# Weight conversion with signs made on GpSimd, and a first output product in two passes

## The chip, the cores and the metric

The kernel runs on one core of a Trainium2 chip. The metric is the device time of one execution in microseconds (us). A core has five engines that work side by side, each through its own queue in order: TensorE (PE) multiplies matrices, VectorE (DVE) and ScalarE (ACT) work elementwise and can read the banks of PSUM in which TensorE leaves its sums, GpSimd (POOL) works elementwise between tiles of on-chip memory (SBUF), and SyncE (SP) issues DMAs.

## The reference

Eight batches of twelve heads, 448 tokens and head size 64 go through attention with normalised queries and keys, and the result, as 3584 rows of 768, through a gated feed-forward layer with 1536 hidden values. The three weight matrices come as 64-bit floats.

```python
q_n, k_n = rmsnorm(q, g_q), rmsnorm(k, g_k)
attn = softmax(q_n @ k_n.T / sqrt(64))
x = (attn @ v).transpose(0, 2, 1, 3).reshape(3584, 768)
g = x @ w_gate                       # 768 x 1536
silu = g * (1.0 / (1.0 + exp(-g)))
out = (silu * (x @ w_val)) @ w_out   # 1536 x 768
```

## The kernel before

The work is cut into four blocks of two batches. A block has twelve pairs of heads (m = 0 to 47 in all, `attention`, L703), a hidden product (gate and value) and an output product (`block`, L1267).

**Products.** Each large product is done by a bilinear scheme on 3 x 3 sub-blocks by 15 products in place of 18 per two batches. Both factors are first combined into 15 "sides": sums and differences of blocks. The hidden product of a block runs over four groups g of hidden columns, and within each over the 15 products x in the order `UP_ORDER`, for gate and value, each two terms deep (`up_product`, L1280). Every product is left in a PSUM bank and read from there at once, by ScalarE if it opens a sum (COPY) and by VectorE if it is added to or subtracted from one (L1242 to L1248). The bank is free for the next product when that read is done. The output product (`down_product`, L1452) has the 15 products of `DOWN_ORDER`, for two halves s of the columns, each four terms deep: its terms are the groups g. Two banks serve it, one for each s. Its data sides are made by `combine` (L1425) from the hidden values in `gt` into the tiles `gt`, `hs` and two spare slots of `xs`; sums 6 and 1 are made group by group behind the hidden product and wait in block 0 for the last use of `hs` by a conversion. The data sides of the hidden product are made in `xs` by `sides` (L1042), after the last pair of a block's half.

**Weights.** Twenty-four pieces of weights, 16 for the hidden product (four to a group) and 8 for the output product (two to a group), are converted by `convert` (L1101). A piece is 128 x 1152 64-bit numbers. It is loaded into one of nine places, which are tiles not needed yet (`gt`, `hs`, `es`, `xs`, `work` of the pairs' inputs, `spare`); ScalarE scales the high word into a 32-bit number (L1127) and turns the low word into a correction (L1131); VectorE rounds in two halves of three operations each (`round_part`, L1138): a shift (L1147), the sign bit masked out of the high word and joined (L1150), and the correction added (L1153). GpSimd makes the sums among the blocks in twelve operations (L1171, L1174), and the 15 sides are stored to DRAM (L1199), in `up_sides` per group or in `down_sides`. From there SP loads them piece by piece into two `ws` buffers just ahead of TensorE (`load_sides`, L1250). With `by_bank` the results of the first two vector operations go to a PSUM bank of the pool `st` instead of back to SBUF. The pieces are handed out in rounds (L1586 on): 6 in the first round, during the first twelve pairs, then 10, 6 and 2, all planned before the end of block 0's hidden product. Each round walks over its own list of places, and a place is taken again when its store has landed. Pairs 12 and on use `work` and `es`, so their loads wait for the last conversion in `work` and their scores for the last in `es`.

**Order.** The order in which instructions stand in the engines' queues comes from a planner (`Order`, L361). Every piece of work is added with an engine, an expected duration, a due time (`when`), what it must follow, and buffers that it takes. `run` (L422) keeps a clock for each engine in this model and places at each step the piece that could start first, by due time among those close together. `port=True` keeps VectorE and GpSimd pieces from being planned at the same time. Due times come from a few numbers at L636: the first pair at `LEAD` = 14 us and each of the first twelve at a distance `PAIR` = 10 us, then block 0's hidden product with 20 us of extra room, and so on. What really happens follows the queues and the semaphores, not the due times.

The first twelve pairs run before block 0, and the twelve of a next block run between the output product's pieces of the block before. Pairs need TensorE for scores (L840), weighted values (L916) and row sums (L940); the early ones also to spread the reciprocals (L980).

Of the kernel before, what the change touches and what calls it, by code (L numbers as in the profile page):

```python
# [9 lines left out]
F32 = mybir.dt.float32  # L10
# [467 lines left out]
def fast(  # L478
# [87 lines left out]
    def take(name, key, shape):  # L566
# [4 lines left out]
        if name in OFTEN:  # L571
            at = OFTEN[name] + order.turn[name] % BUFS[name]
            tiles[name, key] = spare[:, ts(at, S)]
            return tiles[name, key]
        if name == "eh":
            at = order.turn["eh"] % BUFS["eh"]
            tiles[name, key] = more[:, at].rearrange("p (h q) -> p h q", h=2)
            return tiles[name, key]
# [35 lines left out]
    down_sides = dram.tile([P, 15, 2, NG, P], F32, name="down_sides")  # L614
# [21 lines left out]
    LEAD, PAIR = 14.0, 10.0  # L636
# [66 lines left out]
    def attention(m):  # L703
# [296 lines left out]
        def divide():  # L1000
# [4 lines left out]
            "ACT", 0.55, when + 3.0, copy_sums, after=[last, up_done.get(b // 2 - 1)], uses=at[:1]  # L1005
# [36 lines left out]
    def sides(n, c, when):  # L1042
# [7 lines left out]
        for i, one, two, op in (  # L1050
# [13 lines left out]
            free = down_products.get((n - 1, 11), []) if i in (11, 12) else []  # L1064
            last = [
# [35 lines left out]
    def convert(key, src, sums, to, when, place, by_bank):  # L1101
# [9 lines left out]
        wait = [last_exp[0]] if place in (ES, PAIRS, GT[2]) else []  # L1111
# [21 lines left out]
        )  # L1133

# [3 lines left out]
        def round_part(k, takes=False):  # L1138
            if by_bank:
                if k == 0:  # L1140
                    take(*bank, [P, 2, TB])
                part = ts(k, VALUES // 2)
                to = tiles[bank].rearrange("p b t -> p (b t)")[:, 0 : VALUES // 2].bitcast(U32)
            else:
                part = ts(k, VALUES // 2)
                to = bits[:, part]
            nc.vector.tensor_scalar(  # L1147
                out=to, in0=bits[:, part], scalar1=3, scalar2=None, op0=ALU.logical_shift_left
            )
            nc.vector.scalar_tensor_tensor(  # L1150
                to, hi[:, part], 0x80000000, to, op0=ALU.bitwise_and, op1=ALU.bitwise_or
            )
            nc.vector.tensor_tensor(out=bits[:, part], in0=to, in1=lo[:, part], op=ALU.add)  # L1153

        last = one
        for k in range(2):
            last = add(
                "DVE", 2.28 if by_bank else 1.85, when, lambda k=k: round_part(k), after=[last, two],
                takes=[bank] if by_bank and k == 0 else [], uses=[bank] if by_bank and k else [],
                port=not by_bank,  # L1160
            )
# [51 lines left out]
    def down_weights(i, *how):  # L1213

        g, s = divmod(i, 2)
        w = moe_w_out.rearrange("(k g p) (n s f) -> p k g n s f", g=NG, p=P, n=3, s=2)
        weights["down", i] = convert(
            ("down", i), lambda k, n: w[:, k, g, n, s], DOWN_SUMS, down_sides[:, :, s, g], *how
        )
# [3 lines left out]
    down_done = {}  # L1223
    last_load = []
# [25 lines left out]
    def load_sides(key, sides, part, sums):  # L1250

        size = 2 * (NC2 if sums is UP_SUMS else NG) * P
        to = take(*key, [P, WS])[:, 0 : len(part) * size].rearrange("p (x f) -> p x f", f=size)
        i = 0
        for names, first in ((sums, 0), (BLOCKS, len(sums))):
            here = sorted(names.index(x) for x in part if x in names)
            if here:
                size = len(here)
                src = sides[:, ds(first + here[0], size)]
                nc.sync.dma_start(to[:, ds(i, size)], src.rearrange("p x a b f -> p x (a b f)"))  # L1260
                i += size
# [5 lines left out]
    def block(n):  # L1267
# [122 lines left out]
        def up_load(g, piece):  # L1390
# [3 lines left out]
                lambda: load_sides(key, up_sides[g], UP_ORDER[5 * piece :][:5], UP_SUMS),  # L1394
# [6 lines left out]
        for g in range(NG):  # L1401
# [5 lines left out]
        up_done[n] = last  # L1407
        bank_read[:] = [free[0, 0], free[0, 1]]
# [3 lines left out]
        raw = [gt[:, :, k] for k in range(6)]  # L1412
        a1, a2, a3, b1, b2, b3 = raw
        h0, h1 = hs[:, 0], hs[:, 1]
# [3 lines left out]
            6: h0, 1: h1, 10: h2, 14: b1, 2: h0, 3: h1, 0: a3, 11: h2, 4: b3, 12: h0, 5: a1, 8: h1,  # L1418
            7: b2, 13: b1, 9: a2,
        }  # L1420
        all_hidden = [hidden[g, k] for g in range(NG) for k in range(6)]
# [3 lines left out]
        def combine(x, one, two, op, when, after, g=None):  # L1425
            to = where[x]
            if g is not None:
                to, one, two = to[:, g], one[:, g], two[:, g]
            done = add(
                "DVE", 0.64 if g is not None else 2.05, when,  # L1430
                lambda: combined(to, one, two, op), after=after, port=True,
            )
            made.setdefault(x, []).append(done)
            return done

        span = (BOTH if n < NB - 1 else DOWN) / 15

        def step_time(x):
            return block_end(n) + DOWN_ORDER.index(x) * span

        for g in range(NG):
            when = start + 30 * (g + 1) * unit + 1.0
            before = [down_done.get(n - 1)] + ([staged[HS]] if n == 0 else [])
            combine(6, a1, a2, None, when, [hidden[g, 0], hidden[g, 1], *before], g)
            combine(1, b2, h0, ALU.subtract, when, [made[6][g], hidden[g, 4], *before], g)
        combine(10, h1, b1, None, block_end(n) + 3.0, [*all_hidden, *made[1], up_done[n]])
# [5 lines left out]
        def down_product(step, x, s):  # L1452
            nonlocal last
            when = step_time(x) + s * span / 2
            piece = step // 2
            key = ("ws", (n, "o", piece))
            size = 2 if piece < 7 else 1
            if piece not in loads:
                loads[piece] = add(
                    "SP", 0.9, when - 24.0,  # L1460
                    lambda: load_sides(key, down_sides, DOWN_ORDER[2 * piece :][:2], DOWN_SUMS),
                    after=[*last_load, *(weights["down", i] for i in range(2 * NG))], takes=[key],
                    kb=512 * size, early=10.0,
                )
                last_load[:] = [loads[piece]]
            fresh = x in FRESH

            def emit():
                w = tiles[key][:, 0 : 4 * NG * P]
                w = w.rearrange("p (x s g f) -> p x s g f", s=2, g=NG, f=P)  # L1470
                at = place_of(x, DOWN_ORDER[step - step % 2 :][:2], DOWN_SUMS)
                for g in range(NG):
                    nc.tensor.matmul(  # L1473
                        banks[s][:, 0:S], w[:, at, s, g], where[x][:, g],
                        start=fresh and g == 0, stop=g == NG - 1, skip_group_check=True,
                    )

            last = add(
                "PE", 2 * PRODUCT, when, emit,
                after=[  # L1480
                    last, loads[piece], bank_read[s], *made.get(x, []),
# [5 lines left out]
            when += 2 * PRODUCT  # L1487
            t, how, *final = DOWN_READ[x]
            name = "vw"[s] + {"t0": "0", "t1": "1", "t4": "2", "t3": "3", "d": "3", "t5": "4"}[t]
            value = (name, (n, "o", t))  # L1490
# [15 lines left out]
            if x == 12:  # L1506
                other = ("vw"[s] + "1", (n, "o", "t1"))
# [7 lines left out]
            if not final:  # L1515
                return
# [24 lines left out]
        for step, x in enumerate(DOWN_ORDER):  # L1541
            when = step_time(x)
            for s in range(2):
                down_product(step, x, s)
            after = {
                6: [(2, b3, b1, ALU.subtract, (1,))],
                1: [(3, h0, a3, ALU.add, (2, 10))],
                10: [(11, a3, b3, ALU.add, ()), (4, b2, b3, None, (2, 11))],
                14: [(13, a2, b2, ALU.add, (2, 10))],
                2: [(12, h1, a1, ALU.subtract, (3,))],  # L1550
                3: [(8, a3, b2, ALU.subtract, (12,)), (9, a2, a3, ALU.add, (6, 13))],
            }.get(x, [])
            for to, one, two, op, others in after:
                combine(
                    to, one, two, op, when + span,
                    [*all_hidden, *products[n, x], *(d for o in others for d in made[o])],
                )
# [28 lines left out]
    turns = [(*XS, *GT[:2], HS, SPARE), (ES, PAIRS, GT[2], SPARE, HS), (ES, PAIRS, HS, SPARE), (ES, HS)]  # L1586
    starts = [LEAD - 4.0, FIRST - 20.0, FIRST + 60.0, FIRST + 110.0]
    spans = [16.0, 8.0, 9.0, 10.0]
    counts = [6, 10, 6, 2]
    todo = iter(first)  # L1590
    for n in range(4):
        for i in range(counts[n]):
            make, index = next(todo)
            make(index, starts[n] + spans[n] * i, turns[n][i % len(turns[n])], n > 0)
# [72 lines left out]
```

## Time and profile before

| | us |
|---|---|
| median of 3 runs | 1500.53 (1499.26 to 1501.53) |
| the profiled execution | 1499.07 |
| its span in the profile | 1497.2 |
| TensorE busy | 1434.6 |
| VectorE busy | 916.9 |
| ScalarE busy | 689.8 |
| GpSimd busy | 408.8 |

How to read it: a row of the slices is a busy share in tenths for 40 equal parts of the span, and PEclk in the same way the clock that TensorE was granted. A line such as `PE mm L1299 <- DVE gt L1248: 9.9, 2, 6.7` says that TensorE's instructions of line 1299 which write `mm` waited for VectorE's of line 1248 which write `gt`, 9.9 us in all, twice, 6.7 at most. A line of the timeline has start, duration, engine, line, operation, tile written and tiles read, shapes, count, and in brackets the idle time before it. Every matmul in 32 bits leaves two records. Stages by TensorE's work: first pairs from 14.66 to 149.3 us, block 0's hidden product to 353.9 and its output product with the next pairs to 526.4; then 717.9 and 872.1 for block 1, 1064.1 and 1218.4 for block 2, 1399.5 and 1485 for block 3, which has no pairs left to run.

### The profile page before, as it was taken

The page shows a single profiled execution, that of the slowest core. Times are in us where ns is not written, and L with a number is a line of the kernel's source. Part 1 is how long each engine was busy: PE and PEld are TensorE (multiplying, and loading weights), DVE is VectorE, ACT ScalarE, POOL GpSimd, SP SyncE. Part 2 cuts the span into 40 slices and gives each one's busy share as a digit, 9 for nine tenths or more (in the row PEclk, how much of TensorE's full clock was granted, in tenths as well). Part 3 has the DMA queues.
Part 4 walks back from the last instruction along what each step waited for, and adds up shares of the span by engine and source line. Part 5 has one row for each costly group of instructions (what it writes and reads, how often), then busy time and mean ns, then how long its engine had stood idle before and what let it go on. Part 6 is the DMA issues. An engine that isn't in the chain of part 4 may idle for free.

```text
span 1497.2 us, 19504 instructions
## 1 busy us (share of the span) xinstructions
PE 1434.6 (96%) x6672; PEld 681.5 (46%) x6672; DVE 916.9 (61%) x1405; ACT 689.8 (46%) x1372; POOL 408.8 (27%) x468
## 2 busy tenths in 40 slices
PE   5898999799999999999999999999999999999998
PEld 2333444343344455554444445554444445555553
DVE  5867877868886743455876753453786854423533
ACT  6764544347777422254777432235677532122100
POOL 2562666544454300002344400002344410000000
PEclk9898999999999999999999999999999999999999
DMA  7675999974444342343453442343344343222235
GB/s 168 152 160 166 315 309 309 288 219 99 98 99 109 80 137 71 114 114 88 100 123 82 87 130 84 104 118 104 82 110 109 83 114 106 71 106 70 84 97 106
DMA packets 415922, 193.31 MB, mean 129 GB/s; under 512 B 324164, under 2 KB 397892, under 8 KB 409668
## 3 DMA queue, kind: packets, MB, share of 16 engines
q1 hardware_dynamic: 402688, 190.35, 47.5%
q10 hardware_dynamic: 12996, 1.61, 0.7%
q8 instruction: 55, 0.90, 0.3%
q14 instruction: 55, 0.45, 0.1%
q0 software_dynamic: 128, 0.00, 0.0%
HBM read 157.29 MB, written 34.60 MB: 128 GB/s over the span
## 4 chain that ended last, share of the span: by engine, by line
PE 73%; DVE 3%; ACT 1%; issue 1%; DMA 0%; SPq 0%; DVEq 0%; ACTq 0%
PE mm L1473 22%; PE mm L1299 19%; PE at L1299 19%; PE st L840 6%; PE at L916 6%; PE st L940 1%; DVE ss L684 0%; DMA out_dram<-spare 0%; ACT es L855 0%; DVE sums L866 0%; DVE ss L768 0%; DVE rd L975 0%; DVE ss L782 0%; DVE hs L1040 0%; ACT spare L990 0%
## 5 line engine op out<-in xcount | busy, mean ns | idle before, releaser
L1299 PE MATMUL mm<-xs,ws 128*128 128x448 f32 x960 | 405.0, 544 | 15.9 <-DVE gt L1248 9.9
L1299 PE MATMUL at<-xs,ws 128*128 128x448 f32 x960 | 400.7, 540 | 0.8 <-DVE v L1246 0.7
L1299 PEld LDWEIGHTS mm<-xs,ws 128*128 128x128 f32 x960 | 182.1, 191 | 199.4 <-issue 169.2
L1299 PEld LDWEIGHTS at<-xs,ws 128*128 128x128 f32 x960 | 182.3, 190 | 182.1 <-issue 174.5
L795 POOL TENSOR_TENSOR work<-work,rr 128x448 f32<-128x448 f32 x96 | 97.8, 1040 | 504.7 <-DVE rr L686 345.6
L1473 PE MATMUL mm<-gt,ws 128*128 128x448 f32 x448 | 175.7, 543 | 0.0
L840 PE MATMUL st<-work 64*64 64x448 f32 (+1 forms) x1536 | 154.8, 510 | 21.9 <-ACT work L814 15.6
L1244 DVE TENSOR_TENSOR gt<-gt,mm 128x448 f32<-128x448 f32 x64 | 39.7, 621 | 210.2 <-PE mm L1299 185.7
L1473 PE MATMUL mm<-hs,ws 128*128 128x448 f32 x384 | 151.0, 544 | 0.0
L855 ACT ACTIVATE es<-st 128x896 f32<-128x896 f32 x129 | 114.5, 915 | 75.5 <-PE at L916 52.2
L1373 ACT ACTIVATE st<-gt 128x448 f32<-128x448 f32 x96 | 52.6, 548 | 204.8 <-DVE gt L1248 104.4
L860 POOL TENSOR_TENSOR sums<-es 128x896 f32<-128x896 f32 x36 | 78.1, 2170 | 193.0 <-PE st L940 84.7
L990 ACT COPY spare<-rd 32x224 f32<-32x224 f32 x288 | 108.2, 376 | 47.3 <-DVE rd L975 42.1
L1473 PEld LDWEIGHTS mm<-gt,ws 128*128 128x128 f32 x448 | 83.5, 190 | 83.4 <-issue 80.5
L916 PE MATMUL at<-es,v 64*64 64x448 f32 x1032 | 115.0, 561 | 4.5 <-DVE xs L998 3.3
L1242 ACT COPY gt<-mm 128x448 f32<-128x448 f32 x80 | 42.6, 532 | 162.5 <-PE mm L1299 162.4
L1473 PEld LDWEIGHTS mm<-hs,ws 128*128 128x128 f32 x384 | 71.3, 190 | 71.4 <-issue 69.6
L840 PEld LDWEIGHTS st<-work 64*64 64x64 f32 x1536 | 52.0, 134 | 98.0 <-issue 35.7
L1242 ACT COPY v<-at 128x448 f32<-128x448 f32 x96 | 51.0, 531 | 76.1 <-PE at L1299 75.9
L860 POOL TENSOR_TENSOR sums<-sums,es 128x896 f32<-128x896 f32 x36 | 75.8, 2107 | 6.7 <-ACT es L855 4.1
L811 DVE STREAM_TRANSPOSE work<-work 128x448 f32<-128x448 f32 x96 | 58.7, 628 | 24.6 <-POOL work L795 15.1
L916 PEld LDWEIGHTS at<-es,v 64*64 64x64 f32 x1032 | 40.9, 138 | 67.7 <-issue 59.2
(141 smaller groups left out, 1581.6 us busy)
## 6 DMA issues: line engine op xcount, KB each, us to landing
ws<-up_sides SPq DMA_DIRECT2D x32, 1024.0 KB, 4.9
ws<-down_sides SPq DMA_DIRECT2D x16, 1024.0 KB, 4.9
ws<-down_sides SPq DMA_DIRECT2D x28, 512.0 KB, 4.0
ws<-up_sides SPq DMA_DIRECT2D x16, 768.0 KB, 4.4
work<-in_q_dram SPq DMA_DIRECT2D x192, 56.0 KB, 2.3
work<-in_k_dram SPq DMA_DIRECT2D x188, 56.0 KB, 2.3
out_dram<-spare SPq DMA_DIRECT2D x168, 56.0 KB, 1.9
v<-in_v_dram SPq DMA_DIRECT2D x96, 96.0 KB, 2.4
```

The costliest lines, as they stand in the source:

```text
L795: nc.gpsimd.tensor_tensor(out=tiles["t", m][:, x], in0=tiles["qk", (m, x)], in1=rr.to_broadcast([P, NC, C]), op=ALU.mult,)
L811: nc.vector.transpose(to, tiles["t", m][:, x].rearrange("p c f -> p (c f)"))
L840: nc.tensor.matmul(st[ds(D * x, D), h, 0:n], tiles["KT", m][rows, ds(P * j + D * of_keys, D)], tiles["QT", m][rows, ds(Q * of_queries, n)] ...
L855: nc.scalar.activation(e, tiles["st", (m, j)][:, :, 0 : S * width(j) // P], AF.Exp)
L860: nc.gpsimd.tensor_tensor(out=to, in0=tiles["e", (m, 0)] if j == 1 else to, in1=e, op=ALU.add)
L916: nc.tensor.matmul(tiles["at", (m, x)][ds(D * h, D), queries], tiles["v", m][rows, j, h], tiles["e", (m, j)][rows, h], start=j == 0, stop= ...
L990: nc.scalar.copy(inv[ds(D * h + C * to, C), ts(x, Q)], tiles["rd", m][ds(D * h + C * x, C)])
L1242: nc.scalar.copy(to, ps)
L1244: nc.vector.tensor_tensor(out=to, in0=old, in1=ps, op=ALU.add)
L1299: nc.tensor.matmul(ps(), w[:, at, which, c], xs[:, SLOT[x], c], start=fresh and c == 0, stop=c == NC2 - 1, skip_group_check=True,)
L1373: nc.scalar.activation(take(*act, [P, 2, TB])[:, 0, 0:S], to, AF.Silu)
L1473: nc.tensor.matmul(banks[s][:, 0:S], w[:, at, s, g], where[x][:, g], start=fresh and g == 0, stop=g == NG - 1, skip_group_check=True,)
```

## The change

**Conversion.** GpSimd makes the sign bit: one operation over the 1152 high words, "less than zero" times 2 to the 31st, written back as an integer. VectorE's half has two operations instead of three, a shift joined with the sign by OR and the addition, and each of the four is a piece of its own for the planner, due 0.77 or 0.9 us instead of 2.28 or 1.85 for a half.

**Rounds.** The first round's pieces are due 13 us apart instead of 16; the third round has the places `es`, `work`, `spare`, `hs`, `spare`, `hs`; the last two pieces (group 3 of the output product) are converted in two places of `xs` after block 0's hidden product. `PAIR` becomes 9, so all later due times are 12 us earlier.

**Output product of block 0.** It runs in two passes: all 15 products over groups 0 and 1, then all over groups 2 and 3, each product two terms deep. The second pass adds to the first one's sums. The difference `d` of the first pass is kept apart (`v5`, and `w5` in a free slot of `xs`) and subtracted in the second. Sides are combined for two groups at a time. In all blocks `down_sides` becomes two DRAM tensors of two groups each, so that a `ws` load takes from both, or in a pass from one, four products to a load. A side of the next block in `xs` waits for the late conversions, and the last pair of block 1 for the use of `w5`.

```diff
-    LEAD, PAIR = 14.0, 10.0
+    LEAD, PAIR = 14.0, 9.0
...
+        three = add(
+            "POOL", 1.6, when,
+            lambda: nc.gpsimd.tensor_scalar(
+                out=hi, in0=hi.bitcast(F32), scalar1=0.0, scalar2=2.0**31, op0=ALU.is_lt,
+                op1=ALU.mult,
+            ),
+            after=[one], port=True,
+        )
...
-            nc.vector.tensor_scalar(
-                out=to, in0=bits[:, part], scalar1=3, scalar2=None, op0=ALU.logical_shift_left
-            )
             nc.vector.scalar_tensor_tensor(
-                to, hi[:, part], 0x80000000, to, op0=ALU.bitwise_and, op1=ALU.bitwise_or
-            )
+                to, bits[:, part], 3, hi[:, part],
+                op0=ALU.logical_shift_left, op1=ALU.bitwise_or,
+            )
+
+        def round_part(k):
+            part, to = half(k)
             nc.vector.tensor_tensor(out=bits[:, part], in0=to, in1=lo[:, part], op=ALU.add)
...
         for k in range(2):
-            last = add(
-                "DVE", 2.28 if by_bank else 1.85, when, lambda k=k: round_part(k), after=[last, two],
+            for x, op in enumerate((shift, round_part)):
+                last = add(
+                    "DVE", 0.77 if by_bank else 0.9, when, lambda k=k, op=op: op(k),
+                    after=[last, two, three], ...
...
+        if n == 0:
+            for make, index, when, place in late_weights:
+                make(index, when, place, True, [last])
...
+        passes = [(0, 2), (2, 4)] if n == 0 else [(0, NG)]
...
-                for g in range(NG):
+                size = 2 * 2 * P * len(part)
+                at = place_of(x, part, DOWN_SUMS)
+                side = place(p, x)[1]
+                for g in range(hi - lo):
+                    w = tiles[key][:, ds(g // 2 * size, size)]
+                    w = w.rearrange("p (x s g f) -> p x s g f", s=2, g=2, f=P)
                     nc.tensor.matmul(
-                        banks[s][:, 0:S], w[:, at, s, g], where[x][:, g],
-                        start=fresh and g == 0, stop=g == NG - 1, skip_group_check=True,
+                        banks[s][:, 0:S], w[:, at, s, g % 2], side[:, g],
+                        start=fresh and g == 0, stop=g == hi - lo - 1, skip_group_check=True,
                     )
...
+            if sums_too and how == COPY:
+                how = ADD if t in ("t1", "t3") else FROM
...
+                if p:
+                    c3 = ("vw"[s] + "5", (n, "o", "d", 0))
+                    drained[s, "d"] = add(
+                        "DVE", 0.64, when + 1.5,
+                        lambda: nc.vector.tensor_tensor(
+                            out=tiles[value], in0=tiles[value], in1=tiles[c3], op=ALU.subtract
+                        ),
+                        after=[drained[s, "d"]], uses=[value, c3], port=True,
+                    )
...
-    turns = [(*XS, *GT[:2], HS, SPARE), (ES, PAIRS, GT[2], SPARE, HS), (ES, PAIRS, HS, SPARE), (ES, HS)]
-    starts = [LEAD - 4.0, FIRST - 20.0, FIRST + 60.0, FIRST + 110.0]
-    spans = [16.0, 8.0, 9.0, 10.0]
+    turns = [(*XS, *GT[:2], HS, SPARE), (ES, PAIRS, GT[2], SPARE, HS), (ES, PAIRS, SPARE, HS, SPARE, HS), XS]
+    starts = [LEAD - 4.0, FIRST - 20.0, FIRST + 60.0, block_end(0)]
+    spans = [13.0, 8.0, 9.0, 12.0]
```

## The prediction

> **What bounds the kernel now.** First the page's busy shares and its 40 slices of 37.4 us:
>
> ```profile
> PE 1434.6 (96%) x6672; PEld 681.5 (46%) x6672; DVE 916.9 (61%) x1405; ACT 689.8 (46%) x1372; POOL 408.8 (27%) x468
> ...
> PE   5898999799999999999999999999999999999998
> ...
> PEclk9898999999999999999999999999999999999999
> ```
>
> TensorE is the bound, and what it loses is lost early: the digits below 9 and the low clock stand almost all in the first nine slices. So I cut the span where TensorE changes work, by the windows view (columns: width, busy us and count of PE, PEld, DVE, ACT, POOL, then clock, DMA share, GB/s):
>
> ```profile
> 14.66:149.30 134.64, 115.21 (x1201) 49.27 (x1202) 93.95 (x157) 85.96 (x165) 60.16 (x91) 0.91 0.68 166
> 149.30:353.90 204.60, 188.84 (x506) 92.36 (x505) 159.68 (x244) 97.68 (x138) 118.60 (x224) 0.97 0.89 272
> 353.90:526.40 172.50, 168.19 (x1082) 72.61 (x1080) 135.09 (x185) 114.58 (x257) 75.39 (x44) 0.99 0.45 100
> 526.40:717.90 191.50, 191.50 (x601) 95.01 (x601) 90.23 (x155) 68.51 (x128) 11.54 (x10) 1.00 0.36 105
> 717.90:872.10 154.20, 154.20 (x985) 70.56 (x986) 113.41 (x163) 101.02 (x229) 63.41 (x38) 1.00 0.45 100
> ```
>
> The rows are the first twelve pairs, block 0's hidden product, block 0's output product with the next twelve pairs, then the same two stages of block 1. Block 1 needs 191.5 + 154.2 = 345.7 us and TensorE never idles; block 0 needs 377.1. So block 0 loses 31.4 us. Of this the hidden stage has 21.5: its 480 matmul records at the warm 0.376 us (four start every 1.504 us in the timeline) are 180.5, the pair work in it 2.6, and 204.6 - 183.1 = 21.5 (15.8 idle, 5.7 slow clock). The output stage has the other 9.9. The first twelve pairs lose more, but by latency: their warm matmuls make about 8.0 us a pair, 96 of 134.6.
>
> Whom TensorE waits for in the hidden stage (total, times, longest):
>
> ```profile
> PE mm L1299 <- DVE gt L1248: 9.9, 2, 6.7
> PE mm L1299 <- DVE gt L1244: 4.1, 2, 2.2
> PE mm L1299 <- DVE xs L1036: 0.9, 1, 0.9
> PE at L1299 <- DVE v L1246: 0.7, 1, 0.7
> ```
>
> All of it is VectorE, reading a PSUM bank late. VectorE's timeline around the longest one shows why:
>
> ```profile
> 292.60 0.75 DVE L1147 TENSOR_SCALAR st<-work 128x576 uint32<-128x576 uint32 x1
> 293.44 0.76 DVE L1150 SCALAR_TENSOR_TENSOR st<-work,st 128x576 uint32<-128x576 uint32 x1
> 294.32 0.76 DVE L1153 CUSTOM_DVE_ANT_0 work<-work,st 128x1152 uint16<-128x1152 uint16 x1
> 295.11 0.76 DVE L1147 TENSOR_SCALAR st<-work 128x576 uint32<-128x576 uint32 x1
> 295.91 0.76 DVE L1150 SCALAR_TENSOR_TENSOR st<-work,st 128x576 uint32<-128x576 uint32 x1
> 296.71 0.75 DVE L1153 CUSTOM_DVE_ANT_0 work<-work,st 128x1152 uint16<-128x1152 uint16 x1
> 297.38 0.62 DVE L1248 TENSOR_TENSOR gt<-mm,gt 128x448 f32<-128x448 f32 x1
> ```
>
> The read that frees the bank stands behind one weight conversion of six pieces, 4.8 us long; TensorE restarts at 298.05.
>
> **What the Trainium skill says.** "SBUF — State Buffer", Who interferes with whom: a vector instruction with two SBUF inputs and a GpSimd instruction that reads SBUF exclude one another for the whole instruction; with one SBUF input it doesn't contend. The trace agrees: L1150 with one input in PSUM takes 761 to 774 ns in all 36 cases, with both in SBUF (first stage) up to 1169. "VectorE: DVE Perf Modes", The perf-mode tier table: a 32-bit `tensor_scalar` runs double rate from SBUF to SBUF and single rate with PSUM. Agrees: L1147 takes 453 and 755 ns. "TensorE: Matmul & The Clock Gate", HAM oscillation: idle gaps beyond about 3.4 us cost the clock. Here less is enough: after 2.48 us idle at 46.8 us, eight matmuls took 1.77 instead of 0.98 us.
>
> **The change part by part.**
>
> 1. *Conversions, vector side.* Six pieces a conversion become four: the shift takes the sign by OR, the masking piece is gone. In the hidden stage a conversion falls from 6 x 0.755 = 4.53 to 4 x 0.76 = 3.04, but the shift now reads two SBUF operands while GpSimd is 58% busy there (118.6 of 204.6). Free contention is 0; the first stage's worst is 0.4; I take 0.3 for each of two, so 3.65. The pieces are also queued singly, so a read can come between them. Sixteen instead of eighteen conversions fall in the stage: VectorE has 18 x 4.53 - 16 x 3.65 = 23 us less, 159.7 to 137.
> 2. *Signs on GpSimd.* One `tensor_scalar` over 1152 values each. The trace has none. "GPSIMD Engine Reference", 3.1 and 7, gives 1.03 cycles an element at 1.2 GHz for one or two operations, 2.03 for an unpaired compare, 2.9 for a wide stride: estimates of 1.0, 1.95 and 2.8 us. I take 1.95. It is hidden as long as GpSimd has room: 118.6 - 2 x 6.5 (a conversion's twelve sums, 162.15 to 168.6) + 16 x 1.95 = 137 of about 193. Without cover it is on the chain, because the vector piece waits for it, and the bank reads stand behind that piece in order.
> 3. *Hidden stage.* The bursts of conversion pieces behind L1248 and L1246 (10.6 idle, and most of the 5.7 of slow clock that follow the two long gaps) should mostly go. The wait of 2.2 at 326 us stays: it comes from six combinations in a row that wait for the last use of the `hs` place (322.5 to 330), still an item of the last round. The 1.9 at 275 stand behind conversions too, but some bursts will still meet. So I leave 10 of 21.5: -11.5. Bounds: -16 if little but the 2.2 and the 0.9 stay, -3 if GpSimd's signs hold VectorE up.
> 4. *First twelve pairs.* The planner's pitch goes from 10 to 9 us; the measured one is 134.6 / 12 = 11.2. A due time moves nothing by itself. What does is six conversions: in SBUF they take about 2 x (0.52 + 0.87 + 0.84) = 4.5 and then 2 x (0.87 + 0.84) = 3.4 us of VectorE, 6 us in all, in finer grains. TensorE waits there for VectorE's L684 (5.7), L975 (4.2) and L998 (1.1). I take -4, from 0 to -12 (one us a pair).
> 5. *Output stage of block 0.* Matmuls are the same 240 records. Each sum over four terms becomes two over two, so 60 products of 1.5 us with a read each stand for 30 of 3.0. VectorE: 16 reads become 16 + 28 (pass two adds where it copied, but for `d`), +28 x 0.62 = 17.4; two more additions `t1 + d` and two subtractions of the first pass's `d`, 2.5; nine combinations of 2.02 become eighteen of about 1.1, +1.6; two late conversions, 7.3. That is +29. Against it, the `es` and `work` places are let go after the first two items of their round instead of near the end, so pairs 12 and 13 can be prepared in the hidden stage, as in block 1, whose output stage needs 113.4 of VectorE against 135.1 here. 113 + 29 = 142 of 165 to 172: 84%. The loss at its start (2.1, 0.5 and 0.7 us idle between 372 and 416, with the slow clock after) I put at -6; the bank reads with half the slack at +6. Sum 0, between -8 and +20.
> 6. *Moved DMAs.* Two conversions' loads and stores, 2 x (1152 + 960) KB, leave a stage where DMA is 89% busy for one at 45%. They need hidden data only in the second pass, half a stage later. SP issues for later blocks' `ws` loads roughly double from two to four a load, 0.42 us each; in block 1 these come every 20 us. Nothing on the path.
> 7. *Blocks 1 to 3, tail.* Same matmuls; TensorE full there: 0.
>
> Sum: -4 - 11.5 + 0 = -15.5 against the profiled execution, 1499.07 (span 1497.2 and 1.9 around it): 1483.6. The median shown, 1500.53, lies 1.5 above, so 1485.
>
> **Rivals.**
>
> *Slower: VectorE becomes the bound of the output stage.* If the pairs aren't prepared earlier, it has 135 + 29 = 164 us. From 380 to 415 it ran at 30.35 of 35, 87%, and TensorE already waited; 164 / 0.86 = 191, +18.5. With half the gains of 3 and 4 (-8) this ends at +10.5: 1511; with all of them at 1503.5. It decides from an output stage over 188 us. For it: a bank's read has 1.5 us to hide in, and a reciprocal (1.55) or a combination ahead uses that up. Against it: pair matmuls of 2.6 us stand between the products.
>
> *The signs are late.* At 2.8 us GpSimd has 151 of 193 in the hidden stage, VectorE waits in order, half of the bursts' gain is lost and the first stage gains nothing: about -5, 1495.5, or no measurable change.
>
> *Everything falls into place:* the first stage reaches 10.2 us a pair (-12), hidden -15, output -4: -31, 1469.5.
>
> **How the numbers follow.** Forecast 0.45 (own range 1477 to 1493), late signs 0.17, everything 0.18, slower 0.20. A difference under 0.2% (3 us) is about what measuring can't tell from none. Faster: 0.45 + 0.18 + 0.13 of the late signs = 0.76; within: 0.04 + 0.03 = 0.07; slower 0.17. The range runs from the foot of "everything", 1469, to the middle of the slower case, 1506, leaving out some 0.1 at each end.
>
> **What would show it.** Right: the L1248 wait under 4 us; hidden stage near 193; first up product near 145; output stage 168 to 176 with VectorE over 80%. Wrong: TensorE waiting for reads of the output stage over 15 us in sum, VectorE waiting for GpSimd's sign, signs over 2.5 us, or the first stage no shorter.

## The result, and the profile after

The changed kernel takes 1576.62 us (median of 4 runs, 1571.18 to 1578.3) against 1499.89 of the kernel before in the same session: a ratio of 1.0513, 95% interval 1.0473 to 1.0553. It is 77 us slower; 15 faster was forecast, and the range ended at 1506.

Busy shares and slices of the changed kernel's page:

```profile
PE 1466.5 (93%) x6672; PEld 689.5 (44%) x6672; DVE 945.5 (60%) x1398; ACT 697.3 (44%) x1380; POOL 520.2 (33%) x492
...
PE   4788978889698998999999999999999999999998
...
PEclk9988989999899989999999999999999999999999
```

GpSimd has 111 us more, VectorE 29 more, although each conversion now has four vector operations instead of six. TensorE's thin part now reaches to the sixteenth slice (39.4 us each here). The stages by TensorE's work, in the windows view with the columns as before (the first twelve pairs, block 0's hidden product, its output product, block 1's hidden product):

```profile
14.74:159.90 145.16, 119.30 (x1201) 52.37 (x1202) 98.51 (x145) 86.30 (x165) 88.72 (x100) 0.88 0.66 158
159.90:391.40 231.50, 201.59 (x530) 96.82 (x529) 149.51 (x201) 99.17 (x145) 182.48 (x216) 0.93 0.76 229
391.40:596.20 204.80, 180.17 (x1058) 72.98 (x1057) 162.25 (x224) 113.03 (x245) 91.01 (x66) 0.93 0.37 89
596.20:796.00 199.80, 193.38 (x601) 95.56 (x599) 95.84 (x164) 73.77 (x138) 11.53 (x10) 0.98 0.39 106
```

Against 134.6, 204.6, 172.5 and 191.5 these are +10.5, +26.9, +32.3 and +8.3, in sum 78.0 of the span's 79.3. All later stages are within 1 us of before. In the hidden stage GpSimd is busy for 182.5 of 231.5 us, 118.6 of 204.6 before.

What TensorE waits for in that stage:

```profile
PE at L1322 <- DVE v L1265: 9.6, 2, 4.8
PE mm L1322 <- DVE gt L1265: 9.5, 2, 7.1
PE mm L1322 <- DVE gt L1269: 5.0, 2, 4.5
PE at L1322 <- ACT v L1263: 4.9, 1, 4.9
```

Still late bank reads, but more of them, and they no longer stand behind six conversion pieces. The timelines of VectorE, GpSimd and TensorE around one of the waits:

```profile
196.32 4.38 DVE L1164 SCALAR_TENSOR_TENSOR st<-gt 128x576 uint32<-128x576 uint32 x1 [5.24 <-POOL gt L1143]
200.62 0.61 DVE L1265 TENSOR_TENSOR v<-v,at 128x448 f32<-128x448 f32 x1
```

```profile
192.07 4.22 POOL L1143 TENSOR_SCALAR gt<-gt 128x1152 uint32<-128x1152 f32 x1
196.26 4.18 POOL L1143 TENSOR_SCALAR spare<-spare 128x1152 uint32<-128x1152 f32 x1
```

```profile
201.28 3.31 PE L1322 MATMUL at<-xs,ws 128*128 128x448 f32 x4 [4.85 <-DVE v L1265]
```

L1143 is the sign, 4.2 us. VectorE first stands idle 5.24 us for the sign in `gt`. Then its shift, 0.76 us of work, takes 4.38: it starts at 196.32, just after the next sign (in `spare`, 196.26), and ends after that one. The bank read L1265 is next in VectorE's queue, and TensorE waits 4.85 us and restarts at half speed (3.31 for 1.67). The longest wait (7.13 us, until 262.04) looks the same: VectorE idle for 5.13 us until a sign is done, then a shift of 4.39. In the whole run VectorE waits for signs eight times, 38.8 us in all.

### The profile page after: what moved, and what is told of

Its sections match the earlier page's. It is cut to its first block, busy times and chain, and to the rows that moved or that the text cites. A ratio compares the mean times of both kernels' runs of the same rounds, so it can differ in the third digit from the quotient of the medians.

```text
span 1576.5 us, 19539 instructions
## 1 busy us (share of the span) xinstructions
PE 1466.5 (93%) x6672; PEld 689.5 (44%) x6672; DVE 945.5 (60%) x1398; ACT 697.3 (44%) x1380; POOL 520.2 (33%) x492
## 4 chain that ended last, share of the span: by engine, by line
PE 66%; DVE 5%; ACT 2%; DMA 1%; SPq 1%; issue 1%; DVEq 0%; ACTq 0%
PE mm L1536 20%; PE at L1322 17%; PE mm L1322 17%; PE at L920 5%; PE st L844 5%; PE st L944 1%; ACT spare L994 1%; DMA out_dram<-spare 1%; DVE xs L1045 1%; DVE hs L1045 1%; SPq L732 0%; DVE rd L979 0%; SPq L1612 0%; ACT es L859 0%; DVE ss L786 0%
## 5 line engine op out<-in xcount | busy, mean ns | idle before, releaser
L1322 PE MATMUL at<-xs,ws 128*128 128x448 f32 x960 | 409.0, 549 | 14.7 <-DVE v L1265 9.6
L1322 PEld LDWEIGHTS at<-xs,ws 128*128 128x128 f32 x960 | 185.7, 194 | 200.4 <-issue 180.1
L799 POOL TENSOR_TENSOR work<-work,rr 128x448 f32<-128x448 f32 x96 | 101.3, 1075 | 452.6 <-DVE rr L690 327.5
L844 PE MATMUL st<-work 64*64 64x448 f32 (+1 forms) x1536 | 159.8, 511 | 25.1 <-ACT work L818 16.2
L1536 PE MATMUL mm<-gt,ws 128*128 128x448 f32 x448 | 179.8, 549 | 0.5 <-DVE spare L1269 0.3
L1536 PE MATMUL mm<-hs,ws 128*128 128x448 f32 x384 | 154.3, 549 | 0.5 <-ACT w L1263 0.5
L920 PE MATMUL at<-es,v 64*64 64x448 f32 x1032 | 126.9, 570 | 28.5 <-DVE xs L1002 25.5
L1265 DVE TENSOR_TENSOR gt<-gt,mm 128x448 f32<-128x448 f32 x64 | 39.7, 620 | 186.7 <-PE mm L1322 186.7
```

The source lines that it names most:

```text
L799: nc.gpsimd.tensor_tensor(out=tiles["t", m][:, x], in0=tiles["qk", (m, x)], in1=rr.to_broadcast([P, NC, C]), op=ALU.mult,)
L844: nc.tensor.matmul(st[ds(D * x, D), h, 0:n], tiles["KT", m][rows, ds(P * j + D * of_keys, D)], tiles["QT", m][rows, ds(Q * of_queries, n)] ...
L920: nc.tensor.matmul(tiles["at", (m, x)][ds(D * h, D), queries], tiles["v", m][rows, j, h], tiles["e", (m, j)][rows, h], start=j == 0, stop= ...
L1265: nc.vector.tensor_tensor(out=to, in0=old, in1=ps, op=ALU.add)
L1322: nc.tensor.matmul(ps(), w[:, at, which, c], xs[:, SLOT[x], c], start=fresh and c == 0, stop=c == NC2 - 1, skip_group_check=True,)
L1536: nc.tensor.matmul(banks[s][:, 0:S], w[:, at, s, g % 2], side[:, g], start=fresh and g == 0, stop=g == hi - lo - 1, skip_group_check=True,)
```

## The experiments

Two theories at first. A: the sign's price on GpSimd is the whole loss. B: the sign lengthens the first two stages, and the two passes the output stage. All ratios are to the kernel before on the same chip; stages in us, from TensorE's timeline in the profiled execution of each run:

| run | median | ratio | first pairs | hidden 0 | output 0 | hidden 1 |
|---|---|---|---|---|---|---|
| before | | 1 | 134.6 | 204.5 | 172.6 | 191.4 |
| changed kernel | 1576.6 | 1.0513 | 145.2 | 231.5 | 204.8 | 199.8 |
| signs_only | 1553.3 | 1.0386 | 147.2 | 242.0 | 176.6 | 191.5 |
| passes_six | 1504.2 | 1.0052 | 136.7 | 203.8 | 174.6 | 199.9 |
| honest_plan | 1570.6 | 1.0498 | 134.7 | 260.6 | 180.9 | 197.7 |
| grain | 1493.5 | 0.9970 | 132.0 | 199.5 | 172.9 | 186.0 |
| unsigned | 1493.9 | 0.9974 | 129.0 | 196.8 | 177.3 | 185.9 |
| unwaited | 1533.4 | 1.0250 | 137.4 | 228.0 | 177.6 | 192.0 |
| late_vector | 1563.9 | 1.0449 | 141.9 | 230.9 | 195.8 | 197.5 |
| late_bare | 1555.5 | 1.0372 | 145.7 | 231.2 | 186.3 | 197.8 |
| free_sign | 1514.6 | 1.0108 | 135.4 | 197.9 | 187.1 | 197.7 |
| no_store | 1506.0 | 1.0046 | 135.2 | 200.7 | 174.7 | 199.8 |
| grain_pitch | 1495.3 | 0.9977 | 133.0 | 200.8 | 174.2 | 191.5 |

In grain and unsigned the next pairs' work is shared differently between block 1's stages: hidden and output together are 347.1 and 347.5, against 345.6 before. One stage of one execution is only good to some 3 us: in passes_six and no_store, whose edits differ only behind these stages, the first two differ by 1.5 and 3.1, and in price, which adds work only in block 3, the first three stages are 1.4 to 1.9 shorter than in the kernel before. The profiled execution of passes_six was its slowest, 1512.0 us.

**One part alone: signs_only.**

```diff
 # the kernel before, with the new conversion
+        three = add("POOL", 1.6, ...)    # the sign
...
+            for x, op in enumerate((shift, round_part)):
```

> The kernel before with the new conversion alone (sign on GpSimd, four vector pieces); order of rounds, pitch and output product as before. Theory A, the sign's price: one sign takes 4.24 us of GpSimd where the planner reckons 1.6, and that alone makes the loss, in the output stage too: 1550 to 1570 us. Theory B, the passes: the sign accounts for the first two stages only (10.5 + 26.9 us lost there), the output stage's 32 and the 8 after it belong to the two passes: about 1537 us, with the output stage of block 0 at 172 us as before.

1553.3 us, interval of the ratio 1.0364 to 1.0408. The time is theory A's, the output stage (176.6) theory B's: neither as written. The new conversion alone, its vector savings included, makes 3.86 of the 5.13%. Of the 54 us that its profiled span is longer, 50 are in the first two stages and 4 in the output stage.

**The other part alone: passes_six.**

```diff
 # the changed kernel, signs on VectorE
-        three = add("POOL", 1.6, ...)
...
-            for x, op in enumerate((shift, round_part)):
+            for x, op in enumerate((shift, sign, round_part)):
```

> The changed kernel with signs on VectorE again (the three old operations a half, each a piece of its own for the planner); two passes, late conversions, rounds and pitch as changed. Theory A: the two passes are about neutral, 1490 to 1508 us, output stage of block 0 at 165 to 178. Theory B: 1530 to 1545 us, output stage above 195.

1504.2 us, interval 1.0034 to 1.007. Theory A's side: alone, the passes cost little, 2 us in the output stage and 8.5 in block 1's hidden stage. The two parts alone add up to 4.4%, and both together are 5.13%, some 11 us more. By stages the meeting is larger: the output stage is 26 us longer than the two parts' sum would make it, and the first two stages are 14 us shorter (in the changed kernel two of the conversions have left the hidden stage).

**The plan told the truth: honest_plan.**

```diff
-            "POOL", 1.6, when,
+            "POOL", 4.3, when,
```

> The changed kernel, but the planner is told 4.3 us for a sign instead of 1.6, nothing else. If the loss is the wrong plan (instructions queued behind a sign that the planner thought was over), this takes back most of it: under 1530 us. If it is the work itself on GpSimd and its hold on shared reads, it stays within 15 us of the changed kernel: 1560 to 1580.

1570.6 us, interval 1.0477 to 1.052: the loss isn't the wrong plan. The first stage is back at 134.7, the output stage at 180.9, and the hidden stage takes 260.6 instead. Part of this is pair work that changed places: TensorE has 626 records in the hidden stage, 530 in the changed kernel. Hidden and output stage together take 441.5 us, 436.3 there. So the loss shows up in another stage when the order of the queues changes.

**The price by itself: price.** Twelve GpSimd operations on scratch in block 3:

```diff
+    priced = [
+        op(odd.bitcast(U32), odd, (0.0, 2.0**31), ALU.is_lt, ALU.mult),
+        op(flat.bitcast(U32), flat, (0.0, 2.0**31), ALU.is_lt, ALU.mult),
+        op(flat, flat, (0.0, 1.0), ALU.is_lt, ALU.mult),
+        op(odd, odd, (1.0,), ALU.mult),
+        op(flat, flat, (1.0,), ALU.mult),
+        op(flat, flat, (0.0,), ALU.is_lt),
+    ]
```

> The kernel before with twelve GpSimd operations on scratch added in block 3, where GpSimd is idle: over 128x1152 each twice, first the sign as changed (compare, multiply, written as integers, every second word), then the same on adjacent words, then the same with float output, then one multiply on every second word, one multiply on adjacent words, one compare on adjacent words. If the sign's 4.24 us come from sharing with VectorE, the first takes under 2.5 us here. If they are its own, it takes 4.2, and the others tell which part: stride, integer output, or the second operation. Time as before, 1500 us.

The groups of GpSimd's operations, by form, in short windows of that run; the mean of one in ns is the number behind the busy time:

```profile
L1607 POOL TENSOR_SCALAR es<-es 128x1152 uint32<-128x1152 f32 x4 | 17.1, 4294 | 4.5 <-PE at L916 4.3
```

```profile
L1607 POOL TENSOR_SCALAR es<-es 128x1152 f32<-128x1152 f32 x2 | 8.6, 4317 | 0.2
```

```profile
L1607 POOL TENSOR_SCALAR es<-es 128x1152 f32<-128x1152 f32 x2 | 6.5, 3252 | 0.1
```

The first are the signs on every second and on adjacent words, the second the same with float output, the third single operations. So 4.2 us is the sign's own price. The second operation is 1 us of it; stride and integer output are nothing. The six single operations took 3.1 to 3.3.

This run brought a surprise. Its one execution took 1514.6 us, not 1500: block 3's hidden stage lasted 201.4 instead of 181.2. The operations ran back to back, just when VectorE had to make the sides for block 3's first products, and these sums have two operands in SBUF. The same six sums, in the timeline of the kernel before (block 1) and of this run (block 3):

```profile
527.51 3.54 DVE L1040 TENSOR_TENSOR xs<-xs 128x448 f32<-128x448 f32 x6
```

```profile
1227.98 17.86 DVE L1040 TENSOR_TENSOR xs<-xs 128x448 f32<-128x448 f32 x6
```

0.6 us each became 3.0: every one stood behind a GpSimd operation of 3 to 4.5 us.

**Finer pieces: grain.** The old three operations, six single pieces for the planner, in the kernel before:

```diff
-            last = add(
-                "DVE", 2.28 if by_bank else 1.85, when, lambda k=k: round_part(k), ...
+            for x, op in enumerate((shift, sign, round_part)):
+                last = add("DVE", 0.77 if by_bank else 0.8, when, ...
```

> The kernel before with its three vector operations a half put to the planner as six single pieces instead of two; the same operations, signs on VectorE. If bank reads waited because conversions stood in the queue as blocks of three, the hidden stage of block 0 falls from 204.5 to 192 to 198 us and the whole to about 1490. If it is the sum of vector work, nothing changes: within 4 us of before.

1493.5 us, interval 0.996 to 0.9981, hidden stage 199.5: outside the 192 to 198 that blocks in the queue were to bring, and the whole gained 3.3 us of some 7: the blocks account for about half at most. One wait of 8.1 us for a bank read remains. This kernel is faster than both the changed one and, by 0.3%, the one before.

**No sign at all: unsigned.** signs_only without GpSimd's operation:

```diff
-        three = add("POOL", 1.6, ...)
...
-                to, bits[:, part], 3, hi[:, part],
+                to, bits[:, part], 3, zero.bitcast(U32).to_broadcast([P, VALUES // 2]),
```

> The kernel before with the new four vector pieces and no sign at all: GpSimd's operation is left out and the OR takes a zero, so all weights come out positive. What the saved vector work is worth if the sign cost nothing. By the prediction's steps 3 and 4, about 15 us: 1481 to 1486, hidden stage near 193. If the vector work saved isn't on the path, 1494 to 1500.

1493.9 us, interval 0.9963 to 0.9985. The first two stages fall by 5.6 and 7.7 us, beside the 4 and 11.5 of the prediction. But the output stage gives back 4.7 and what follows it some 4, which leaves 4.7 of span. The whole stands at the edge of "not on the path": finer pieces and a third less vector work were together worth 3 us, no more than finer pieces by themselves (grain).

**The sign done, but not waited for: unwaited.** As unsigned, with `three` kept on GpSimd; against signs_only the order reads:

```diff
-                    after=[last, two, three], ...
+                    after=[last, two], ...
```

> As the run without a sign, but GpSimd still does its 4.24 us operation for each conversion and nobody uses what it writes, so VectorE doesn't wait for it (weights positive again). If VectorE's wait for the sign is what cost the 57 us, this is near the run without a sign, at most 12 us above. If GpSimd's time is (its later sums come late, and reads of two on-chip operands stand behind its operation), this stays within 15 us of the signs alone: 1540 to 1560.

1533.4 us, interval 1.0223 to 1.0276, between the two expectations. By subtraction, 39.5 us over unsigned are GpSimd's time as such, and the remaining 20 to signs_only VectorE's wait. One part of the 39.5 can be read off: the 36 shifts of the hidden stage take 48.9 us of VectorE here and 30.6 in unsigned, 18 us more, though nothing waits for the sign. GpSimd is busy for 200.8 of 228.0 us in the hidden stage. TensorE's longest sum of waits there is for weights:

```profile
PE mm L1312 <- DMA ws<-up_sides: 11.5, 4, 3.6
PE mm L1312 <- DVE gt L1257: 5.9, 4, 2.2
PE mm L1312 <- DVE gt L1261: 5.9, 4, 2.0
```

A group needs four conversions in 45 us of products; by an estimate from the 6.5 us of a conversion's sums and the 4.2 us of a sign they take GpSimd 43.

**Where the parts meet: late_vector and late_bare.** In the changed kernel, the signs of the two late conversions on VectorE; then no sign and no vector piece for these two at all:

```diff
+        late = place in XS and by_bank
+        if not late:
             three = add("POOL", 1.6, ...)
...
 # late_bare only
-            for x, op in enumerate((shift, round_part)):
+            for x, op in enumerate(() if late else (shift, round_part)):
```

> The changed kernel with the signs of the two late conversions made on VectorE as before; the other 22 stay on GpSimd. If the output stage's 32 us come from the two late signs (4.3 and 5.1 us of GpSimd at its start, with 3 to 5 us combinations on VectorE beside them), that stage falls from 205 to below 185 us and the whole to about 1550. If they come from the two passes together with the late start, it stays above 195 us.

> The changed kernel in which the two late conversions have neither a sign nor any vector piece (their weights are wrong); loads, ScalarE's part, GpSimd's sums and stores stay. If TensorE's longest wait of the output stage (for the join of a pair's two halves, 11.6 us with the late signs and 8.3 without) is the join standing behind the late conversions' vector pieces in VectorE's queue, that wait falls below 3 us and the stage to 180 to 188. If not, the stage stays at 194 or more.

Output stage 195.8 and 186.3, from 204.8. The first is not below 185 but above 195, on the side of "two passes together with the late start"; the second is in its range. TensorE's waits in the output stage, changed kernel, late_vector, late_bare:

```profile
PE at L920 <- DVE xs L1002: 18.9, 4, 11.6
```

```profile
PE at L920 <- DVE xs L1002: 12.7, 4, 8.3
```

```profile
PE at L920 <- DVE xs L1002: 1.8, 1, 1.8
```

L1002 joins a pair's two halves and frees the `at` bank. In VectorE's queue it stands behind the eight (or twelve) pieces of the late conversions, and these behind combinations that GpSimd's late signs stretch. VectorE and GpSimd in the changed kernel:

```profile
401.27 3.65 DVE L1045 TENSOR_TENSOR hs<-gt 128x896 f32<-128x896 f32 x1
405.02 2.79 DVE L1045 TENSOR_TENSOR hs<-hs,gt 128x896 f32<-128x896 f32 x1
407.73 4.81 DVE L1045 TENSOR_TENSOR xs<-gt 128x896 f32<-128x896 f32 x1
...
421.48 0.61 DVE L1002 TENSOR_TENSOR xs<-xs,at 128x448 f32<-128x448 f32 x1
```

```profile
400.06 4.26 POOL L1143 TENSOR_SCALAR xs<-xs 128x1152 uint32<-128x1152 f32 x1 [11.93 <-ACT xs L1134]
406.83 5.12 POOL L1143 TENSOR_SCALAR xs<-xs 128x1152 uint32<-128x1152 f32 x1
```

In late_vector the same three combinations take 1.02 to 1.09 us each, as GpSimd has no late signs beside them. So both causes are there: the signs stretch the combinations, and the conversion pieces keep the join waiting. Taking the signs away shortened the stage by 9 us and taking the pieces away by 9.5 more; each edit also changes the order of the queues, so these sizes hold for these orders only. In another order both can stay: TensorE's waits for L1002 in the output stage are 2.0 us in honest_plan, with all 24 signs on GpSimd, and 0.3 in passes_six, with twelve pieces of late conversions.

**Everything but the sign: free_sign.** The changed kernel, edited like unsigned.

> The whole changed kernel without the sign operation: GpSimd's part is left out and the OR takes a zero, so all weights come out positive. If the sign's time on GpSimd is the whole cause, the rest of the change is near the kernel with passes and old signs (1504 us) or a little below: 1488 to 1505, output stage of block 0 under 182 us. If the passes with late conversions cost by themselves, the output stage stays above 190 us.

1514.6 us, interval 1.0091 to 1.0125; the output stage at 187.1 lies between the two expectations. So leaving out the sign takes away 4.05 of the 5.13%, and the rest of the change costs 16 us even then, and 20 to 21 against unsigned. Against passes_six, which makes the sign on VectorE and is alike otherwise, its output stage is 12.5 us longer, although each conversion has two vector pieces fewer. The two stages in the windows view, passes_six first:

```profile
355.10:529.70 174.60, 168.87 (x1057) 70.15 (x1055) 144.81 (x219) 110.63 (x239) 83.65 (x64) 1.00 0.44 104
348.10:535.20 187.10, 174.42 (x1058) 71.44 (x1057) 152.01 (x219) 111.04 (x243) 80.46 (x64) 0.98 0.41 96
```

TensorE is idle for 12.7 us in free_sign, 5.7 in passes_six and 4.3 before, in many short waits (those for VectorE's bank reads are 3.3). The 240 records of the output product take about the same in both, 100.2 and 99.7 us (96.0 before), so the shorter products don't make the difference. The pair matmuls take 89.4 us against 81.5, at a clock of 0.98 against 1.00. The edit also changed the order of the queues; why this order is worse stays open.

**Two smaller questions.**

```diff
 # no_store: passes_six without block 0's stores
-            add("SP", 2.4 if n < NB - 1 else 1.2, when + 1.4, store, ...)
+            if n > 0:
+                add("SP", 2.4 if n < NB - 1 else 1.2, when + 1.4, store, ...)
 # grain_pitch: grain with two numbers of the change
-    LEAD, PAIR = 14.0, 10.0
+    LEAD, PAIR = 14.0, 9.0
...
-    spans = [16.0, 8.0, 9.0, 10.0]
+    spans = [13.0, 8.0, 9.0, 10.0]
```

> The run with two passes and old signs, with block 0's output rows not stored (its output is missing). There block 1's hidden stage is 8.5 us longer than before, and its first product waits 5.2 us for a side that comes late. If that is because the second pass finishes ten of its twelve results close together and their transposes wait for row buffers that the stores hold, the 8.5 us fall to under 3. If the last pair is late for another reason, block 1's hidden stage stays at 197 to 201 us.

199.8, against 199.9 with the stores: they don't make block 1's late start. What the traces show is the cover of the last pair. In the chain of the kernel before, after its last matmuls:

```profile
516.66 0.52 PE st L940 x8
517.18 9.22 PE mm L1473 x24
526.40 1.70 PE mm L1299 x4
```

TensorE has 9.2 us of output products while the last pair is divided and its sides are made. In no_store's timeline the output product's last matmuls (L1533) end at 524.27, before the last pair's row sums (L944). One matmul of block 1 (two records) follows, and then the wait for the side comes bare:

```profile
531.37 1.86 PE L1319 MATMUL mm<-xs,ws 128*128 128x448 f32 x2 [5.18 <-DVE xs L1041]
```

That it is the order left by the two passes is argued only; no run put products back behind the last pair.

> The run with six single pieces, with the pitch of the first pairs at 9 us and the first round's conversions at 13 instead of 10 and 16 as in the change. By step 4 of the prediction the due times move nothing by themselves: within 4 us of the six pieces alone (1493). If the closer pitch helps, the first stage falls from 132 to under 127 us; if it hurts, above 136.

1495.3 us, interval 0.9963 to 0.9991, first stage 133.0: the closer pitch moves nothing by itself.

## Why the prediction was wrong

**Step 2, the sign on GpSimd, failed.** It took 1.95 us from the Trainium skill ("GPSIMD Engine Reference", 3.1 and 7) with 2.8 as its upper end; 4.24 was measured, 4.4 cycles an element at the page's 1.2 GHz, where the page gives 1.03 to 2.9. The bounds were meant to hold an operation that the trace didn't show, and both were the page's. The nearest rows of the trace, sums of two operands at 2.08 us for 896 elements, would have given 2.7 for 1152, too little as well. With 4.24 the step's own sum turns: 118.6 - 13 + 16 x 4.24 = 173 of 193 us is no room to hide in. Measured were 182.5 us of 231.5, and VectorE's 38.8 us of waiting for signs. The step did name what happens then (the vector piece waits, and bank reads behind it).

**Step 1, contention.** 0.3 us a shift was taken, at most 0.4. Without signs this is more than enough: in unsigned, where a zero from SBUF stands for the sign, the 36 shifts of the hidden stage take 0.85 us on average, and VectorE is busy there for 135.9 us where the step says 137. The Trainium skill ("SBUF — State Buffer", Who interferes with whom) says that one side waits for the whole instruction of the other, and the trace agrees: single shifts took up to 4.46 us beside signs of 4.2. A bound read from contention with operations of 0.5 us doesn't hold for one of 4.2. unwaited puts GpSimd's occupation at 39.5 us; the 18 us of longer shifts are part of it, but how much of the 39.5 is the lock and how much the late sums isn't told apart.

**Step 3, hidden stage:** -11.5 forecast, +26.9 measured; without the sign -7.7 (unsigned) and -6.6 (free_sign). Bursts of conversion pieces did cost something, but less than the step took: with six single pieces the stage changes by -5.0 (grain), -3.7 (grain_pitch), -3.8 (no_store) and -0.7 (passes_six). Of the waits that the prediction shows as late bank reads, the 0.9 us for L1036 is a combination. **Step 4, first pairs:** -4 forecast, +10.5 measured; without the sign -5.6 (unsigned) but +0.8 in the whole change (free_sign), so its size isn't confirmed. That the pitch moves nothing was right.

**Step 5, output stage:** 0 forecast within -8 and +20, +32.3 measured. With signs on VectorE it is +2.0 (passes_six), near the forecast, with VectorE busy for 144.8 us where the step says 142; so its sum holds with the passes and the late conversions but without the sign on GpSimd. (It counts 16 vector reads in a pass, the kernel has 18; the 28 added ones are right.) In the changed kernel TensorE waits for a pair's join, behind the late conversions, which the step priced as 7.3 us of vector work with no regard to what stands behind them in the queue. Without any sign it is +14.6 (free_sign), within the bounds but not by the named mechanism: half the slack for bank reads cost 3.3 us of waits. **Step 7,** nothing in later blocks, missed 8.3 us in block 1's hidden stage, where the last pair has no output products behind it as cover. **Step 6,** no transfer on the path, holds in the changed kernel: none of the waits of TensorE in these two stages names a DMA.

**The rivals.** "The signs are late" named the right mechanism and the wrong size: it gave -5 us in all, where signs_only measured +57, because it put the sign at 2.8 us and let the vector savings stay. "VectorE becomes the bound of the output stage" gave the right sign: it asked for over 188 us, and the stage took 204.8. But VectorE was busy for 162 of these, 79%, and TensorE's long wait there came from what stood ahead of the join in VectorE's queue, not from a full VectorE.

## What to carry to other kernels

Before work is moved to an idle engine, measure that one instruction there: GpSimd was busy for 27% of the span here, but in the stage that needs the weights it was busy for 58%, and the added operation took this to 79% (88% in unwaited). Price also what a long GpSimd instruction does to every vector operation with two SBUF operands beside it. And price late work on an in-order engine by what stands behind it in the queue, not only by its own duration. Putting the pieces to the planner singly brought 3 us, and a third less vector work on top of that nothing measurable.

## What was not expected of the hardware

- A GpSimd `tensor_scalar` with one operation over 128x1152 takes 3.1 to 3.3 us, with two about 4.3 (price), whatever the stride of one or two words and whether it writes floats or integers. Per element (2.7 to 2.8 and 3.7 ns) that is more than a sum of two operands (2.08 us for 896 elements, 2.3 ns).
- Under back-to-back GpSimd operations of 3 to 4.5 us, vector sums of two SBUF operands ran one to each of them: six took 17.86 us instead of 3.54. Bank reads and transposes beside them kept their 0.6 us.
